# Attention, a token mixer and two feed-forward stages on one core: widening's transfers on GpSimd's queue, and seven weight slabs in attention

## The chip, the core and the metric

The kernel runs on one core of a Trainium2 chip. The metric is the device time of one execution in microseconds (us). Before the change the median of three runs was 990.18 us (990.01 to 993.89). The engines are called TensorE (PE in the rows), VectorE (DVE), ScalarE (ACT), GpSimd (POOL) and SyncE (SP). SP computes nothing, and its queue issues transfers. A row called PEld is TensorE's weight load, which runs beside its matmuls.

## What is computed

The reference is a random-feature attention, a token mixer with a first MLP, and a Fourier mixer with a normalised second MLP. Cut to what matters:

```python
# attention: q, k, v are (4, 8, 576, 64), omega is (128, 64)
phi(x) = exp(h - max(h)) / sqrt(128),  h = x @ omega.T - |x|^2 / 2,  x = x / 64 ** 0.25
kv, z  = sum over s of phi(k) v,  sum over s of phi(k)
x      = (phi(q) kv) / (phi(q) z + 1e-6)                  # as (4, 576, 512)
# mixer and first MLP: w_ch1 is (512, 1536), w_ch2 is (1536, 512)
u      = x + (relu(x^T w_tok1) w_tok2)^T
y      = u + relu(u w_ch1) w_ch2
# Fourier mixer and second MLP: (512, 2048) and (2048, 512)
u      = y + real(fft over features of fft over tokens of y)
out    = u + relu(norm(u) w_ch1') w_ch2'
```

The weights of the token mixer and of both MLPs arrive as 64-bit floating point numbers. The engines work in 32 bits, so the kernel first turns each weight into a high and a low 32-bit part. This step is called widening.

## The kernel before

**Stages.** Attention works through 72 slots, one for each half of a tile of 128 tokens of k or q. In a slot TensorE projects (line 411), VectorE takes a maximum (the reduce of line 425) and ScalarE an exponential (429, 433). Three slots later TensorE adds a k tile to its sums (445) or transposes a q tile (464), and later forms the quotient's numerator (482), which VectorE divides (491 to 505). Once all q tiles of a batch are through, the token mixer's pieces run in the slots as filling: two long ones (15 matmuls each, line 570, and VectorE's line 574 behind them) and eight short ones (line 583, and VectorE's line 586). Seven more slots let the pipeline run out. Then come five blocks of the first MLP (`ch_block`, 12 steps each) and five of the second (`ff_block`, 16 steps each). A step multiplies up (12 matmuls, line 691), takes the relu and its low part (lines 772 and 773) and multiplies the step before down (12 matmuls, line 812 or 1117).

**Weights.** There are 12 slabs of the first MLP and 16 of the second, each 1 MB in and 1 MB out. Widening takes a slab through seven VectorE instructions and one of ScalarE: `take` (273), the scaling on ScalarE (280), `rest` (284), `size` (288), `high` (292), `low` (296), `unit` (300) and `scaled` (304). A load brings a slab from DRAM into one of two buffers (`stg`, line 262). A store takes the result from one of two buffers (`cvo`) to DRAM (`kept`, line 335). A step of an MLP block then loads the slab from there (`w<-kept`, `refill`, line 660) into one of five places, some three steps before it is needed. Four chunks of the token mixer's weights go through the same widening ahead of the slabs.

**The order.** It is written out by hand: each engine runs its instructions in the order in which the program emits them, and each queue its transfers. `Side.step(budget)` stands at the end of every slot and every MLP step. It adds a budget, in microseconds, to a credit and emits widening instructions as long as the credit covers their listed price (6.38 for a slab). `Side.later` puts off a load or store by `defer` steps, four in attention and one after it. All these transfers, and the loads of q, k, v and the slabs, are on SP's one queue, in which a transfer that waits holds up all behind it.

Of the kernel before, what the change touches and what calls it, by code (L numbers as in the profile page):

```python
# [9 lines left out]
F32 = mybir.dt.float32  # L10
# [22 lines left out]

SLOT0_US, SLOT1_US, SLOT_US, FIRST_US, SHORT_US, CH_US, FF_US, SAVED_US = 0.4, 0.65, 0.85, 4.2, 1.2, 3.9, 3.9, 4.5


LAG, LAG_NUM, LAG_X, AHEAD_LOAD, AHEAD_SPLIT, DEFER = 3, 5, 7, 6, 4, 4
# [145 lines left out]
class Side:  # L185
# [10 lines left out]

    def later(self, fn, steps=None):
        due = self.steps + (steps or self.defer)
        k = sum(d <= due for d, _ in self.issues)
        self.issues.insert(k, (due, fn))  # L200

# [33 lines left out]
def mix_kernel(ctx: ExitStack, tc: tile.TileContext, qt, kt, va, om, w1, w2, wch, wff, t1, t2, out):  # L235
    nc = tc.nc
    pe, act, dve, pool, sync = nc.tensor, nc.scalar, nc.vector, nc.gpsimd, nc.sync
# [13 lines left out]
    def widen(src, n, done):  # L251
# [4 lines left out]
        st = {}  # L256
# [2 lines left out]

        def load():  # L260
            st["w"] = cv.tile([128, 2048], I32, tag=f"stg{k}", name="stg")
            sync.dma_start(out=st["w"][:, 0:2 * n], in_=src)

        def take():
            while "w" not in st or k in busy:
# [37 lines left out]
        def scaled():  # L303
            dve.scalar_tensor_tensor(out=st["o"][:, 1, 0:n], in0=st["l"].bitcast(F32), scalar=2.0 ** -52,
                                     in1=st["y"], op0=ALU.mult, op1=ALU.mult)

        f = n / 1024
        return (load, lambda: (done(st), busy.remove(k))), [
            (w * f, fn) for w, fn in ((0.68, take), (0.68, rest), (0.69, size), (1.21, high), (1.21, low), (0.69, unit),
                                      (1.22, scaled))]  # L310
# [18 lines left out]
    kept = {}  # L329
    whole = set()  # L330

    def slab(ff, j):
        def store(st):
            kept[ff, j] = dram.tile([128, 2, 1024], F32, name="kept")
            sync.dma_start(out=kept[ff, j], in_=st["o"].bitcast(F32))
            whole.add((ff, j))
        return widen((wff if ff else wch)[j].bitcast(I32), 1024, store)

# [40 lines left out]
    src = {}  # L379
# [227 lines left out]
        qn, kn = qe, ke  # L607

    side = Side()

    fill = []
    early = []
# [146 lines left out]
    p0.close()  # L759
    ps0.close()  # L760
    pools["S"] = ctx.enter_context(tc.tile_pool(name="ps_s", bufs=2, space=PSUM, reuse_waits="tile")), 2
    side.defer = 1


    hp = ctx.enter_context(tc.tile_pool(name="hp", bufs=2, reuse_waits="tile"))
# [404 lines left out]
```

## Time and profile before

| | before |
|---|---|
| median of three runs | 990.18 us |
| the profiled execution | 989.0 us, of which the span is 987.2 us |
| TensorE busy | 954.3 us (97%) |
| VectorE, ScalarE, GpSimd busy | 551.7, 277.0 and 78.4 us |
| attention with its run-out | the first 210.4 us |
| first block of the first MLP | 210.4 to about 299 us |

The span runs from the first to the last instruction. Busy time is what an engine's instructions took, waits not counted. TensorE is busy nearly all the time, so a change of the whole time shows as a change of TensorE's idle time, or of its clock, or of how many matmuls it is given. The releaser of an idle time is the work whose end let the engine go on.

### The profile page before, as it was taken

What the parts mean: (1) busy time and instruction counts of PE and PEld (TensorE: products, weight loads), DVE (VectorE), ACT (ScalarE), POOL (GpSimd) and SP (SyncE); (2) the same over time, 40 slices, a digit from 0 to 9 for tenths busy, and PEclk for the clock granted to TensorE, in tenths of its full rate; (3) what the DMA queues carried; (4) which work ended last, traced back from release to release, by engine and by line L of the source; (5) the groups of instructions that cost most, each with busy time, mean ns of one, the idle gap of its engine ahead of it and who ended that gap; (6) DMA issues with size and microseconds to landing.
All of it is one profiled execution on the core that took longest, in us unless ns stands there. A gap on an engine that the chain in (4) does not pass through costs nothing.

```text
span 987.2 us, 13163 instructions
## 1 busy us (share of the span) xinstructions
PE 954.3 (97%) x5248; PEld 827.6 (84%) x5248; DVE 551.7 (56%) x1055; ACT 277.0 (28%) x621; POOL 78.4 (8%) x68
## 2 busy tenths in 40 slices
PE   7999999999879899999999999999999999999998
PEld 7999989888759887888888888888888888888897
DVE  6997879696655568966786542154336433511221
ACT  6876667532112212221221211111111111111111
POOL 3443334210000000000000000000000000000000
PEclk9999999999979999999999999999999999999999
DMA  8954433377787779548176673024202420251081
GB/s 281 285 199 146 156 128 139 128 280 263 255 275 270 293 277 422 201 167 328 54 273 219 242 289 128 1 88 169 86 1 86 171 86 1 86 192 64 1 321 41
DMA packets 33693, 175.00 MB, mean 177 GB/s; under 512 B 3680, under 2 KB 4064, under 8 KB 15584
## 3 DMA queue, kind: packets, MB, share of 16 engines
q1 hardware_dynamic: 33488, 173.05, 48.2%
q0 software_dynamic: 144, 1.11, 0.4%
q8 instruction: 41, 0.67, 0.3%
q14 instruction: 20, 0.16, 0.0%
HBM read 136.27 MB, written 34.08 MB: 173 GB/s over the span
## 4 chain that ended last, share of the span: by engine, by line
PE 81%; DMA 9%; DVE 7%; ACT 2%; issue 1%; SPq 0%; POOL 0%; DVEq 0%; ACTq 0%; POOLq 0%
PE H L691 32%; PE A L1117 20%; PE A L812 12%; DMA kept<-cvo 5%; PE A L411 3%; PE A L570 2%; PE N L482 2%; PE H L445 2%; DMA w<-kept 2%; PE S L982 1%; DVE mx L425 1%; ACT f L429 1%; DVE x L495 1%; DMA stg<-in_wch_dram 1%; PE S L995 1%
## 5 line engine op out<-in xcount | busy, mean ns | idle before, releaser
L691 PE MATMUL H<-uh,w 128*128 128x512 f32 (+1 forms) x1120 | 345.5, 375 | 13.1 <-DMA w<-kept 12.3
L691 PEld LDWEIGHTS H<-uh,w 128*128 128x128 f32 x1120 | 207.4, 191 | 49.9 <-DMA w<-kept 13.4
L773 DVE SCALAR_TENSOR_TENSOR hl<-H,hh 128x512 fp32r<-128x512 f32 (+1 forms) x140 | 89.0, 636 | 253.7 <-ACT hh L772 253.3
L772 ACT ACTIVATE hh<-H 128x512 fp32r<-128x512 f32 (+1 forms) x140 | 77.7, 555 | 499.4 <-PE H L691 497.3
L691 PE MATMUL H<-ul,w 128*128 128x512 f32 (+1 forms) x560 | 208.2, 372 | 0.0
L1117 PE MATMUL A<-w,hh 128*128 128x512 f32 x576 | 146.9, 391 | 0.0
L1117 PEld LDWEIGHTS A<-w,hh 128*128 128x128 f32 x576 | 106.6, 188 | 21.0
L691 PEld LDWEIGHTS H<-ul,w 128*128 128x128 f32 x560 | 107.0, 191 | 17.1
L812 PE MATMUL A<-hh,w 128*128 128x512 f32 (+1 forms) x480 | 109.2, 370 | 0.0
L812 PEld LDWEIGHTS A<-hh,w 128*128 128x128 f32 x480 | 85.0, 190 | 15.2
L1117 PE MATMUL A<-w,hl 128*128 128x512 f32 x288 | 80.6, 390 | 0.0
L1117 PEld LDWEIGHTS A<-w,hl 128*128 128x128 f32 x288 | 54.1, 188 | 11.4
L429 ACT ACTIVATE f<-A,mx 128x128 f32<-128x128 f32 x204 | 59.1, 388 | 8.5 <-DVE mx L425 8.2
L812 PE MATMUL A<-hl,w 128*128 128x512 f32 (+1 forms) x240 | 59.3, 369 | 2.1 <-DVE hl L773 2.1
L425 DVE TENSOR_REDUCE mx<-A 128x4 f32<-128x512 f32 x71 | 48.1, 682 | 5.9 <-PE A L411 5.6
L812 PEld LDWEIGHTS A<-hl,w 128*128 128x128 f32 x240 | 42.5, 189 | 10.3 <-DVE hl L773 2.9
L280 ACT ACTIVATE cvy<-cvy 128x1024 f32<-128x1024 f32 (+2 forms) x32 | 32.8, 1025 | 44.0 <-DVE cvy L273 44.0
L445 PE MATMUL H<-v,f 128*128 128x65 f32 x320 | 41.3, 273 | 0.8 <-ACT kvs L450 0.6
L292 DVE SCALAR_TENSOR_TENSOR cvo<-cvy,cvo 128x1024 int32<-128x1024 int32 (+2 forms) x32 | 41.7, 1305 | 0.4
L482 PE MATMUL N<-kvs,qpT 128*128 128x65 f32 x320 | 39.9, 270 | 1.7 <-ACT f L429 0.9
L445 PEld LDWEIGHTS H<-v,f 128*128 128x128 f32 x320 | 40.0, 194 | 1.2 <-ACT kvs L450 0.7
L482 PEld LDWEIGHTS N<-kvs,qpT 128*128 128x128 f32 x320 | 38.6, 192 | 2.4 <-issue 1.7
(182 smaller groups left out, 1150.4 us busy)
## 6 DMA issues: line engine op xcount, KB each, us to landing
w<-kept SPq DMA_DIRECT2D x84, 1024.0 KB, 4.9
kept<-cvo SPq DMA_DIRECT2D x28, 1024.0 KB, 9.1
stg<-in_wff_dram SPq DMA_DIRECT2D x16, 1024.0 KB, 8.7
stg<-in_wch_dram SPq DMA_DIRECT2D x12, 1024.0 KB, 5.2
v<-in_va_dram SPq DMA_DIRECT2D x20, 260.0 KB, 3.7
ks<-in_kt_dram SPq DMA_DIRECT2D x18, 256.0 KB, 3.8
qs<-in_qt_dram SPq DMA_DIRECT2D x18, 256.0 KB, 3.4
out_dram<-U SPq DMA_DIRECT2D x16, 256.0 KB, 2.2
```

The lines of the kernel that those rows point to most:

```text
L280: act.mul(out=st["y"], in_=st["y"], mul=2.0 ** -112)
L292: dve.scalar_tensor_tensor(out=st["h"], in0=st["y"].bitcast(I32), scalar=-0x80000000, in1=st["h"], op0=ALU.bitwise_and, op1=ALU.bitwise_or)
L411: pe.matmul(out=pj[:, p_ * 256:p_ * 256 + 256], lhsT=a[:, c, :], rhs=w, start=(n == 0), stop=(n == 2), skip_group_check=True)
L425: dve.tensor_reduce(out=mx, in_=p4, axis=AX.X, op=ALU.max, negate=True)
L429: act.activation(out=f[:, hh], in_=p4[:, hh], func=AF.Exp, bias=mx[:, hh])
L445: pe.matmul(out=kvp[b, g][:, hh * 65:hh * 65 + 65], lhsT=ft["k", i, g][:, hh, :], rhs=src["v", i, int(off > 0)][:, 4 * g + hh, :], start=( ...
L482: pe.matmul(out=nm[:, hh * 65:hh * 65 + 65], lhsT=t[:, hh, :], rhs=kvs[b, g][:, hh, :], start=(c == 0), stop=(c == len(ts) - 1), skip_grou ...
L691: pe.matmul(out=hb[:, 0:n], lhsT=a[:, kk * 128:kk * 128 + 128], rhs=u[:, kk, 0:n], start=(c == 0), stop=(c == 11))
L772: act.activation(out=hh, in_=hb[:, 0:n], func=AF.Relu)
L773: dve.scalar_tensor_tensor(out=hl, in0=hb[:, 0:n], scalar=0.0, in1=hh, op0=ALU.max, op1=ALU.subtract)
L812: pe.matmul(out=acc[i][:, 0:cols], lhsT=a[:, cs], rhs=v, start=(j == 0 and c_ == 0), stop=(j == NCH - 1 and c_ == 2))
L1117: pe.matmul(out=acc[t], lhsT=a[:, t * 128:t * 128 + 128], rhs=w, start=(j == 0 and c_ == 0), stop=(j == NFF - 1 and c_ == 2))
```

## The change

Three things are changed. The budgets of a slot are now 0.7 (first ten slots), 0.4 (up to the 36th) and 1.2 (after it) instead of 0.4, 0.65 and 0.85; the budget of a step of the MLPs is 3.9 in the first block and 3.7 later instead of 4.2 and 3.9, and at most 4.0 is saved up instead of 4.5. Once attention is emitted, widening's loads and stores go to GpSimd's queue. And from there on they are no longer put off: `later` with a `defer` of zero emits at once.

```diff
-SLOT0_US, SLOT1_US, SLOT_US, FIRST_US, SHORT_US, CH_US, FF_US, SAVED_US = 0.4, 0.65, 0.85, 4.2, 1.2, 3.9, 3.9, 4.5
+SLOT0_US, SLOT1_US, SLOT_US, FIRST_US, SHORT_US, CH_US, FF_US, SAVED_US = 0.7, 0.4, 1.2, 3.9, 1.2, 3.7, 3.7, 4.0
...
     def later(self, fn, steps=None):
         due = self.steps + (steps or self.defer)
+        if due <= self.steps:
+            return fn()
...
-            sync.dma_start(out=st["w"][:, 0:2 * n], in_=src)
+            side.queue.dma_start(out=st["w"][:, 0:2 * n], in_=src)
...
-            sync.dma_start(out=kept[ff, j], in_=st["o"].bitcast(F32))
+            side.queue.dma_start(out=kept[ff, j], in_=st["o"].bitcast(F32))
...
     side = Side()
+    side.queue = sync
...
-    side.defer = 1
+
+    side.defer, side.queue = 0, pool
```

TensorE's instructions stand in the same order in both kernels. Line numbers after the change are higher by 2 to 4. Names end in a number that counts emissions.

**SP's queue in the first block of the first MLP.** Before, from the loads of slabs 2 to 5 on:

```order
L660 DMA w_2870<-kept_2826 128x2048
L262 DMA stg_2881<-in_wch_dram 128x2048
L335 DMA kept_2883<-cvo_2667 128x2048
L660 DMA w_2918<-kept_2883 128x2048
L262 DMA stg_2995<-in_wch_dram 128x2048
L335 DMA kept_2997<-cvo_2831 128x2048
L660 DMA w_3034<-kept_2997 128x2048
L262 DMA stg_3045<-in_wch_dram 128x2048
L335 DMA kept_3047<-cvo_2941 128x2048
L660 DMA w_3083<-kept_3047 128x2048
```

After, the same place:

```order
L337 DMA kept_2758<-cvo_2343 128x2048
L663 DMA w_2892<-kept_1929 128x2048
L663 DMA w_2894<-kept_2118 128x2048
L663 DMA w_2896<-kept_2339 128x2048
L663 DMA w_2898<-kept_2547 128x2048
L663 DMA w_2944<-kept_2758 128x2048
L663 DMA w_3005<-kept_2856 128x2048
L663 DMA w_3059<-kept_2910 128x2048
L663 DMA w_3110<-kept_2974 128x2048
```

Before, each slab's load from `kept` stood between the store of that slab and the store of the next; now only loads from `kept` are left in the row.

**GpSimd's queue behind attention.** Before, one transfer (the Fourier tables) followed the last subtraction of attention:

```order
L512 TENSOR_TENSOR xl_2633<-x_2623,xh_2632 128x512
L512 TENSOR_TENSOR xl_2708<-x_2698,xh_2707 128x512
L512 TENSOR_TENSOR xl_2768<-x_2758,xh_2767 128x512
L845 DMA t2_sb_3410<-in_t2_dram 128x2176
L1166 UNCONDITIONAL_BRANCH
```

After, the loads (`stg`) and stores (`kept`) of widening stand there, 40 in all:

```order
L514 TENSOR_TENSOR xl_2726<-x_2716,xh_2725 128x512
L514 TENSOR_TENSOR xl_2790<-x_2780,xh_2789 128x512
L264 DMA stg_2854<-in_wch_dram 128x2048
L337 DMA kept_2856<-cvo_2551 128x2048
L264 DMA stg_2861<-in_wch_dram 128x2048
L337 DMA kept_2910<-cvo_2794 128x2048
L264 DMA stg_2971<-in_wch_dram 128x2048
L337 DMA kept_2974<-cvo_2859 128x2048
```

They moved here from SP; the first store on this queue is that of the eighth slab.

**VectorE in attention, slots 48 to 50.** The instructions of widening are those with `cvo` or `cvy` on the left. Before:

```order
L425 TENSOR_REDUCE mx_1637<-A_1620 128x4
L425 TENSOR_REDUCE mx_1675<-A_1650 128x4
L292 SCALAR_TENSOR_TENSOR cvo_1494<-cvy_1493,cvo_1494 128x1024
L586 TENSOR_TENSOR x2_652<-A_1688,x2_652 128x288
L425 TENSOR_REDUCE mx_1709<-A_1698 128x4
L432 TENSOR_TENSOR df_1712<-A_1698,mx_1709 128x512
L296 SCALAR_TENSOR_TENSOR cvo_1494<-cvo_1494,stg_1379 128x1024
L425 TENSOR_REDUCE mx_1736<-A_1718 128x4
```

After:

```order
L427 TENSOR_REDUCE mx_1637<-A_1620 128x4
L294 SCALAR_TENSOR_TENSOR cvo_1530<-cvy_1529,cvo_1530 128x1024
L427 TENSOR_REDUCE mx_1674<-A_1649 128x4
L298 SCALAR_TENSOR_TENSOR cvo_1530<-cvo_1530,stg_1456 128x1024
L588 TENSOR_TENSOR x2_657<-A_1689,x2_657 128x288
L427 TENSOR_REDUCE mx_1710<-A_1699 128x4
L434 TENSOR_TENSOR df_1713<-A_1699,mx_1710 128x512
L302 TENSOR_SCALAR cvy_1529<-cvo_1530 128x1024
L275 TENSOR_SCALAR cvy_1719<-stg_1686 128x1024
L427 TENSOR_REDUCE mx_1740<-A_1722 128x4
```

In the same three slots two instructions of widening became four. Counted over VectorE's whole order, widening has 7 instructions before the eleventh reduce, 27 from there to the 37th, and 40 from there to the first MLP's first relu before the change, and 12, 19 and 56 after it; a slab is seven of them.

## Rows read from the trace of the kernel before

**Rows 1.** The page: busy us, share of the span and instructions by engine.

```profile
PE 954.3 (97%) x5248; PEld 827.6 (84%) x5248; DVE 551.7 (56%) x1055; ACT 277.0 (28%) x621; POOL 78.4 (8%) x68
```

**Rows 2.** Busy us (instructions) by stretch; last TensorE's granted clock, DMA share, GB/s.

```profile
core 0: us, PE busy (x) PEld busy (x) DVE busy (x) ACT busy (x) POOL busy (x), PEclk, DMA share, GB/s
0.00:26.80 26.80, 21.13 (x159) 20.57 (x159) 19.03 (x29) 17.22 (x47) 9.76 (x13) 1.00 0.82 284
26.80:85.30 58.50, 55.83 (x456) 54.67 (x457) 50.13 (x93) 46.85 (x131) 26.55 (x22) 0.97 0.71 225
85.30:210.40 125.10, 118.77 (x916) 112.70 (x916) 100.62 (x208) 80.08 (x192) 41.28 (x32) 1.00 0.40 145
210.40:299.00 88.60, 79.09 (x342) 65.32 (x341) 55.88 (x75) 15.61 (x23) 0.52 (x2) 0.92 0.80 280
```

**Rows 3.** TensorE's waits for transfers: 210.5 to 300 us, then 300 to 345 us.

```profile
PE H L691 <- DMA w<-kept: 9.5, 3, 3.7
...
PE H L691 <- DMA w<-kept: 2.8, 2, 1.7
```

**Rows 4.** TensorE in order of time (start, us; idle before): steps 8 to 11.

```profile
259.51 0.40 PE L691 MATMUL H<-uh,w 128*128 128x512 f32 x1
...
262.25 1.98 PE L812 MATMUL A<-hh,w 128*128 128x512 f32 x8
...
269.38 0.80 PE L691 MATMUL H<-uh,w 128*128 128x512 f32 x1 [3.45 <-DMA w<-kept]
...
274.66 2.45 PE L812 MATMUL A<-hh,w 128*128 128x512 f32 x8
...
281.22 0.51 PE L691 MATMUL H<-uh,w 128*128 128x512 f32 x1 [2.40 <-DMA w<-kept]
...
285.49 2.17 PE L812 MATMUL A<-hh,w 128*128 128x512 f32 x8
...
293.04 0.80 PE L691 MATMUL H<-uh,w 128*128 128x512 f32 x1 [3.67 <-DMA w<-kept]
...
297.30 0.42 PE L583 MATMUL S<-w2hl,h1h 128*128 128x288 f32 x2
```

**Rows 5.** SP's queue in order of time (start and us of the issue).

```profile
240.20 0.32 SPq L660 DMA_DIRECT2D w<-kept  x1
...
241.09 0.38 SPq L335 DMA_DIRECT2D kept<-cvo  x1
252.88 0.32 SPq L660 DMA_DIRECT2D w<-kept  x1
```

**Rows 6.** SP's waits over the span: total us, times, longest.

```profile
SPq L660 <- DMA kept<-cvo: 71.2, 8, 11.6
```

**Rows 7.** VectorE busy (instructions) by stretch, of instructions on `cvo` alone.

```profile
0.00:26.80 26.80, 7.39 (x8) 1.00 0.82 284
26.80:85.30 58.50, 21.28 (x22) 0.97 0.71 225
85.30:210.40 125.10, 37.81 (x34) 1.00 0.40 145
```

**Rows 8.** Chain that ended last (start, us), 85.3 to 210.4 us: widening's first and last.

```profile
92.56 0.87 DVE cvo L284
...
204.88 1.69 DVE cvo L284
```

**Rows 9.** VectorE's longest wait, 85.3 to 210.4 us.

```profile
DVE h1l L574 <- ACT h1h L573: 14.1, 6, 3.5
```

**Rows 10.** VectorE at the start: second reduce, first instruction of widening.

```profile
8.16 0.68 DVE L425 TENSOR_REDUCE mx<-A 128x4 f32<-128x512 f32 x1
11.16 0.50 DVE L273 TENSOR_SCALAR cvy<-stg 128x640 f32<-128x640 f32 x1 [2.31 <-DMA stg<-in_w_dram]
```

**Rows 11.** GpSimd's one transfer: its issue, and (page) us to landing.

```profile
298.56 0.69 POOL L845 DMA_DIRECT2D t_sb<-in_t_dram  x1 [88.08 <-PE S L583]
...
t_sb<-in_t_dram POOLq DMA_DIRECT2D x1, 1088.0 KB, 6.1
```

## The prediction

> **What bounds the kernel now.** I read the table of engines first. TensorE is busy 97% of the span, and its 954.3 us leave 33 us [rows 1]. Its instructions keep their order, so the change can only move those 33 us and the time lost to a lower granted clock. The busy time by stretch then tells where they lie [rows 2] (26.8 and 85.3 us are the eleventh and the 37th reduce, where a slot's budget changes): 5.7 us before 26.8 us (the start), 2.7 us up to 85.3 us, 6.3 us from there to the end of attention at 210.4 us, and 9.5 us in the first block of the first MLP, the one stretch whose granted clock is well below full, 0.92. TensorE's waits name the last: three waits for a slab, 9.5 us in all, the longest 3.7 us, and two more in the second block, 2.8 us [rows 3].
>
> TensorE in order of time shows what such a wait costs beyond itself [rows 4]. Twelve matmuls up take 2.74 us in step 8 (259.51 to 262.25). Behind the three waits the same twelve take 5.28, 4.27 and 4.26 us: the clock has fallen to its lower level, 1.2 GHz, in the idle time, and is back at 2.4 GHz some microseconds later. That is 2.54 + 1.53 + 1.52 = 5.6 us more.
>
> Why the slabs are late is in SP's queue [rows 5]. At 240.20 us it issues a slab's load; the load of new weights and the store of the next slab follow, at 241.09 us. The next entry loads that very slab, so it waits until the store has landed, and goes at 252.88 us: 11.8 us later. The store behind it can't go sooner. So one slab comes every 11.8 us, where a step without a wait takes 6.4 us (259.51 to 269.38, less the wait of 3.45 [rows 4]). SP stood 71.2 us, in eight waits, in this way [rows 6].
>
> **The change part by part.**
>
> *The queue.* GpSimd's queue takes the stores and the loads of new weights; SP keeps the loads from `kept`. GpSimd has nothing else to do by then (0.52 us busy in that block [rows 2]). A slab's load may still wait for its store on SP, but no store waits behind it. By the order, the load of slab 11 is now emitted in step 7 and not in step 10, slab 10 in step 6 and not 9, slab 9 in step 5 and not 7. Four steps of 6.4 us lie between slab 11's load and its use, against an 11.8 us store and a load.
>
> *Slabs sooner.* When the first relu of the MLP is emitted, widening has done 87 instructions against 74. Thirteen more of seven each are 1.9 slabs, or 22 us of head start at the old pace. That is more than the 9.5 us by which the slabs are late. So either part alone nearly cures the three waits, and I take them as gone: -9.5 us, and -5.6 us for the clock. In the second block GpSimd's transfers compete with seven slab loads in 12 short steps. The 2.8 us may go or stay; I take half, -1.4 us.
>
> *What it costs in attention.* Thirteen more instructions of widening are on VectorE there, and they aren't spread evenly. An instruction on `cvo` takes 7.39 / 8 = 0.92 us in the first stretch, 21.28 / 22 = 0.97 us in the second and 37.81 / 34 = 1.11 us in the third [rows 7].
>
> First stretch: 12 instead of 7, +4.6 us on a VectorE with little idle time once the weights are there. And the first of them now stands ahead of the second reduce. It waits for its weights until 11.16 us, while that reduce ran at 8.16 us [rows 10]; the reduce would end at about 12.3 us instead of 8.84, 3.4 us later. TensorE is three slots ahead of what it needs from the reduces, which covers part. Ends: nothing, and 4.6 + 3.4 = 8.0 us. I take +2.5 us, nearer to nothing, since matmuls are queued ahead.
>
> Second stretch: 19 instead of 27, -7.7 us. But TensorE stands only 2.7 us there, and its clock of 0.97 over 58.5 us is 1.8 us more [rows 2]. So between nothing and -4.5 us; I take -2.5 us, about half.
>
> Third stretch: 56 instead of 40, +17.8 us. VectorE is busy 100.6 of 125.1 us [rows 2] and would be at 118.4. It has 24.5 us of idle time, of which 14.1 us are six waits behind the token mixer's long pieces [rows 9]: slack, but in six places. Between them VectorE and TensorE go in step. The chain of waits runs through widening there in 17 pieces, 16.2 us in all, from 92.56 to 204.88 us [rows 8]; 16 more on 40 lengthen these by 0.4, or +6.5 us. Ends: +2 us, if the idle time takes nearly all, and +17.8 us, if none. I take +7.5 us, a little above the scaled chain, because a fuller VectorE is on the chain more often.
>
> Sum: -9.5 - 5.6 - 1.4 + 2.5 - 2.5 + 7.5 = -9.0 us. The profiled execution of 989.0 us would take 980.0 us; its span is 1.8 us shorter than that, and the median of the runs 1.2 us longer. On the median of 990.2 us it is 981.2 us. The rest of the MLPs I cost at nothing: TensorE never waits for a slab there, budgets fall by 0.2, and 1.9 slabs are already done.
>
> A rule weighed against the change: SP's rows show a queue whose head waits while transfers behind it are ready, and here 11.8 us a slab hang on that [rows 5]. The Trainium skill, "DMA: Bandwidth & Descriptors", section "Issuing engines are not separate DMA queues", says that transfers from several engines run on the same 16 DMA engines, and that issuing from several saves only the issue time. By it the move alone would bring next to nothing, and the sum would rest on the head start; the sum is then the same, since 22 us cover the waits.
>
> **The rivals.**
>
> *Attention pays in full.* VectorE's idle time is latency and not slack: each added microsecond delays TensorE. Price: 17.8 + 8.0 - 2.5 = +23.3 us, against 9.5 + 5.6 saved and nothing in the second block: +8.2 us, 998.4 us. It turns slower once attention pays over 15.1 us. For it: the chain passes through widening seventeen times in the third stretch. Against it: the 14.1 us behind the long pieces, and TensorE itself at 118.8 of 125.1 us, so that at present it is VectorE that has the room.
>
> *Attention pays almost nothing.* The six waits and TensorE's own queue take the added work (+2), the start nothing, the second stretch gives 4.5 and the second block 2.8: -9.5 - 5.6 - 2.8 + 2 - 4.5 = -20.4 us, 969.8 us.
>
> *GpSimd's queue is slow.* Each of its transfers waits for VectorE. The one such transfer shown was issued in 0.69 us and landed in 6.1 us for 1.06 MB [rows 11], which speaks against it; but then VectorE wasn't in the midst of widening. Price: with a step's four widening instructions of some 0.92 us (the first stretch's mean) ahead of each transfer, two transfers a slab are 7.4 us late; the last four slabs eat the head start of 22 us and the slack. Part of the three waits returns, some 5 us with their clock: -4 us, 986 us. Where it also starves VectorE of new weights all 15.1 us return: +6 us, 996 us. The Trainium skill, "SBUF — State Buffer", section "SBUF: two separate sides", has this as a trap: while VectorE runs certain fast copies, GpSimd can't write its transfers' descriptors, and such transfers belong on SP's or ScalarE's queue. No row here shows a store from GpSimd.
>
> *The change doesn't do what it says.* Excluded by the order: 40 transfers stand in GpSimd's queue, and slab 11's load is three steps sooner.
>
> **How the numbers follow.** The forecast, with its terms off by some microseconds (976 to 987 us): 0.60. Almost nothing paid: 0.12. Paid in full or nearly (990 to 999 us): 0.14. GpSimd slow (984 to 996 us): 0.14. The range of 8 in 10 runs from 970.5 to 991 us: it holds the forecast, most of the cheap case and the milder half of the other two. A measurement of this kernel tells about 0.5% from no change, so 985.2 and 995.1 us are the bounds. Faster: nearly all of 0.60, 0.12 and a part of the slow queue, 0.72. Slower: over half of the full price, 0.09. Within: 0.19.
>
> **What would show it.** TensorE's waits for slabs in the first two blocks fall from 12.3 us to under 3 us, and the granted clock of the first block is at 0.99 or more. SP no longer waits eight times for a store. Attention ends at about 218 us instead of 210.4, with VectorE at 93% or more in its third stretch. It would be wrong in its main step if attention ended after 226 us, or if the waits for slabs stayed above 5 us, and in its sizes if attention ended before 213 us.

## The result

The changed kernel takes 979.12 us (median of 14 runs, 973.77 to 989.8), the kernel before, on the same chip, 992.07 us (14 runs, 987.04 to 994.4). The ratio is 0.9869, 95% interval 0.9845 to 0.9893: 1.3% faster, some 13 us. Here and below, medians and extremes are over all runs, while the ratios leave out runs over 1.5% above the fastest of the same kernel (two each of the changed kernel, e2 and e8). The forecast was 981.2 us, 9 us under the kernel before. The profiled execution of the changed kernel took 977.99 us, with a span of 975.9 us; before it was 989.0 and 987.2 us.

The page of the changed kernel, first the busy times, to be held against [rows 1]:

```profile
PE 952.6 (98%) x5248; PEld 828.6 (85%) x5248; DVE 549.0 (56%) x1055; ACT 277.1 (28%) x621; POOL 110.3 (11%) x108
```

TensorE does the same 5248 matmuls in nearly the same busy time; GpSimd has 108 instructions instead of 68, the 40 transfers that moved. The span is 11.3 us shorter. I cut both spans at places that can be found in both traces: the first matmul of step 1 of the first block, the first matmul of the second block, that of the third block, and the end. These starts are read from TensorE in order of time.

| stretch | before, us | after, us | difference | forecast |
|---|---|---|---|---|
| start to step 1 of the first block (attention) | 210.43 | 217.91 | +7.5 | +7.5 |
| first block, from step 1 | 93.13 | 76.81 | -16.3 | -15.1 |
| second block | 37.92 | 38.06 | +0.1 | -1.4 |
| from the third block to the end | 645.7 | 643.1 | -2.6 | 0 |
| span | 987.2 | 975.9 | -11.3 | -9.0 |

TensorE's waits of after, from 195 to 345 us (total us, times, longest), answer to [rows 3]:

```profile
PE H L694 <- DMA w<-kept: 2.7, 3, 1.6
```

These three are all in the second block. In the first block there is none. Its stretch in after (us, then busy us of TensorE, of its weight loads, VectorE, ScalarE and GpSimd, then the granted clock, the DMA share and GB/s) is to be held against the last of [rows 2]:

```profile
217.50:297.00 79.50, 79.50 (x385) 67.26 (x384) 58.71 (x83) 16.89 (x28) 14.07 (x17) 1.00 0.83 314
```

In this stretch TensorE is busy 79.50 of 79.50 us at a granted clock of 1.00, where it was 0.92 before.

The waits of SP's queue over the span, which answer to [rows 6], and GpSimd's for a store:

```profile
SPq L663 <- PE A L816: 249.1, 35, 33.5
...
SPq L663 <- DMA kept<-cvo: 24.9, 3, 11.2
```

```profile
POOL kept L337 <- DVE cvo L306: 138.5, 21, 29.8
```

The longest waits of SP's loads of slabs are now for a free place, that is for the matmuls of a slab's last use (L816), 249.1 us, where it was 186.7 before: more slabs are there before they can be loaded. It waits for a store 24.9 us in three waits, where it was 71.2 us in eight. The time that a transfer of widening waits for VectorE has gone to GpSimd, where nothing else stands behind it but the next one of widening.

The transfers by issue (count, KB each, median us from issue to landing) show whether GpSimd's queue costs anything beyond the one transfer of [rows 11]. First after, then before:

```profile
kept<-cvo POOLq DMA_DIRECT2D x21, 1024.0 KB, 7.4
stg<-in_wff_dram POOLq DMA_DIRECT2D x16, 1024.0 KB, 6.5
...
kept<-cvo SPq DMA_DIRECT2D x7, 1024.0 KB, 4.6
```

```profile
kept<-cvo SPq DMA_DIRECT2D x28, 1024.0 KB, 9.1
stg<-in_wff_dram SPq DMA_DIRECT2D x16, 1024.0 KB, 8.7
```

A megabyte from GpSimd lands in 6.5 to 7.4 us, with VectorE widening beside it. From SP's queue before, the same loads took 8.7 us and the stores 9.1, so the move made neither slower. The seven stores that still go from SP, in 4.6 us, are all in attention, where less is moved (a DMA share of 0.40 in its last stretch, against 0.80 in the first block [rows 2]); they can't be held against the 7.4.

### The profile page after: what moved, and what is told of

Its sections match the earlier page's. It is cut to its first block, busy times and chain, and to the rows that moved or that the text cites. A ratio compares the mean times of both kernels' runs of the same rounds, so it can differ in the third digit from the quotient of the medians.

```text
span 975.9 us, 13168 instructions
## 1 busy us (share of the span) xinstructions
PE 952.6 (98%) x5248; PEld 828.6 (85%) x5248; DVE 549.0 (56%) x1055; ACT 277.1 (28%) x621; POOL 110.3 (11%) x108
## 4 chain that ended last, share of the span: by engine, by line
PE 88%; DVE 7%; DMA 2%; ACT 1%; issue 1%; SPq 0%; DVEq 0%; ACTq 0%
PE H L694 35%; PE A L1121 20%; PE A L816 15%; PE A L413 3%; PE N L484 2%; PE H L447 2%; PE A L572 2%; PE S L986 1%; DVE mx L427 1%; DMA w<-kept 1%; DVE x L497 1%; PE S L999 1%; DVE cvo L298 1%; PE S L585 1%; PE S L1105 1%
## 5 line engine op out<-in xcount | busy, mean ns | idle before, releaser
L694 PE MATMUL H<-uh,w 128*128 128x512 f32 (+1 forms) x1120 | 341.1, 371 | 2.7 <-DMA w<-kept 2.7
L694 PEld LDWEIGHTS H<-uh,w 128*128 128x128 f32 x1120 | 205.0, 189 | 37.9 <-DMA w<-kept 3.3
L816 PE MATMUL A<-hh,w 128*128 128x512 f32 (+1 forms) x480 | 108.6, 368 | 0.0
L816 PEld LDWEIGHTS A<-hh,w 128*128 128x128 f32 x480 | 84.3, 189 | 14.8
L816 PE MATMUL A<-hl,w 128*128 128x512 f32 (+1 forms) x240 | 59.1, 368 | 0.0
L816 PEld LDWEIGHTS A<-hl,w 128*128 128x128 f32 x240 | 42.7, 189 | 7.5
L484 PE MATMUL N<-kvs,qpT 128*128 128x65 f32 x320 | 42.4, 280 | 2.6 <-DVE x L507 2.6
L484 PEld LDWEIGHTS N<-kvs,qpT 128*128 128x128 f32 x320 | 41.2, 202 | 3.1 <-POOL ql L401 2.4
L306 DVE SCALAR_TENSOR_TENSOR cvo<-cvo,cvy 128x1024 fp32r<-128x1024 f32 (+2 forms) x32 | 40.0, 1250 | 0.0
L294 DVE SCALAR_TENSOR_TENSOR cvo<-cvy,cvo 128x1024 int32<-128x1024 int32 (+2 forms) x32 | 38.9, 1214 | 0.5
```

Of the source, the lines that this page charges most:

```text
L294: dve.scalar_tensor_tensor(out=st["h"], in0=st["y"].bitcast(I32), scalar=-0x80000000, in1=st["h"], op0=ALU.bitwise_and, op1=ALU.bitwise_or)
L484: pe.matmul(out=nm[:, hh * 65:hh * 65 + 65], lhsT=t[:, hh, :], rhs=kvs[b, g][:, hh, :], start=(c == 0), stop=(c == len(ts) - 1), skip_grou ...
L694: pe.matmul(out=hb[:, 0:n], lhsT=a[:, kk * 128:kk * 128 + 128], rhs=u[:, kk, 0:n], start=(c == 0), stop=(c == 11))
L816: pe.matmul(out=acc[i][:, 0:cols], lhsT=a[:, cs], rhs=v, start=(j == 0 and c_ == 0), stop=(j == NCH - 1 and c_ == 2))
```

## The experiments

In every run the time before was taken again on the same chip: 992.47 us beside e1 to e4, 991.62 beside e5 to e8, 991.36 beside e9 to e12. "Step 1" is the start of the twelve matmuls up of step 1 of the first block, "first block" the time from there to the first matmuls of the second; both, and the waits for slabs in that stretch, are from the profiled execution (e12's is the slowest of its ten). The waits of 10.3 and 16.0 us that the expectations of e5 and e12 name are those of e1 and e4 with the second block's added.

| kernel | median, us (runs) | ratio, 95% interval | step 1, us | first block, us | its waits for slabs, us |
|---|---|---|---|---|---|
| before | 992.07 (14) | 1 | 210.4 | 93.1 | 9.5 |
| after | 979.12 (14) | 0.9869, 0.9845 to 0.9893 | 217.9 | 76.8 | 0 |
| e1: queue alone | 981.88 (4) | 0.9874, 0.9831 to 0.9918 | 212.0 | 85.5 | 7.0 |
| e2: shares alone | 988.48 (10) | 0.9944, 0.9911 to 0.9978 | 217.8 | 82.5 | 2.1 |
| e3: queue alone, put off | 981.61 (4) | 0.988, 0.9837 to 0.9923 | 212.0 | 84.3 | 4.6 |
| e4: at once, on SP | 989.04 (10) | 0.9955, 0.9937 to 0.9974 | 212.3 | 95.1 | 12.8 |
| e5: third share back | 1004.27 (4) | 1.0138, 1.0066 to 1.021 | 215.3 | 101.0 | 17.7 |
| e6: old shares, steeper block | 972.8 (4) | 0.9812, 0.977 to 0.9853 | 209.1 | 79.5 | 1.2 |
| e7: between | 973.97 (4) | 0.9815, 0.9778 to 0.9852 | 215.7 | 76.8 | 0 |
| e8: stores on SP | 988.71 (9) | 0.9957, 0.9929 to 0.9985 | 215.9 | 86.5 | 7.6 |
| e9: three slots free | 974.47 (4) | 0.9823, 0.9789 to 0.9856 | 216.4 | 76.8 | 0 |
| e10: after again | 979.44 (6) | 0.9869, 0.9835 to 0.9903 | 217.8 | 76.8 | 0 |
| e11: e6 again | 974.78 (4) | 0.9833, 0.98 to 0.9866 | 210.4 | 77.5 | 0 |
| e12: e6 on SP | 995.21 (10) | 1.0031, 1.0011 to 1.0052 | 213.3 | 102.3 | 8.3 |

### The two parts apart (e1 to e4)

The change has two parts, the queue (with transfers put off by no step) and the shares. Theory A, that of the prediction, was that either part alone nearly cures the waits in the first block. The first kernel has the queue alone. Against the changed kernel:

```diff
-SLOT0_US, SLOT1_US, SLOT_US, FIRST_US, SHORT_US, CH_US, FF_US, SAVED_US = 0.7, 0.4, 1.2, 3.9, 1.2, 3.7, 3.7, 4.0
+SLOT0_US, SLOT1_US, SLOT_US, FIRST_US, SHORT_US, CH_US, FF_US, SAVED_US = 0.4, 0.65, 0.85, 4.2, 1.2, 3.9, 3.9, 4.5
```

> The old budgets stay, and only the queue and the immediate emission are taken over. Theory A (each part alone nearly cures the late slabs, and the budgets' price is paid in attention): attention ends at about 210 us as before, TensorE waits under 3 us for slabs in the first block, and the time is 15 to 18 us under the kernel before, 6 to 8 us under the changed one. Rival B (the head start does it, the queue is nothing because all transfers share the same engines): the three waits stay near 9.5 us and the time is within 4 us of the kernel before.

Measured: 981.88 us, some 11 us under before, and one wait of 7.0 us left in the first block, for slab 11. That is between Theory A, which had under 3 us of waits and 15 to 18 us, and Rival B. Attention, at step 1, is where it was before, within 2 us. SP, GpSimd and TensorE of this kernel in order of time (start, us; GpSimd's and TensorE's rows end with the idle time before them) show why that one is left:

```profile
268.14 11.62 SPq L663 DMA_DIRECT2D w<-kept  x2
```

```profile
271.85 0.53 POOL L337 DMA_DIRECT2D kept<-cvo  x1 [1.31 <-DVE cvo L306]
```

```profile
287.09 0.79 PE L694 MATMUL H<-uh,w 128*128 128x512 f32 x1 [7.01 <-DMA w<-kept]
```

The slab's store is issued at 271.85 us, 1.31 us after GpSimd began to wait for VectorE. SP issues two loads between 268.14 and 279.76, the second of them when that store has landed. The load lands 7.3 us later. No queue held it up: its widening was finished late. (Its two transfers took their time too, 7.5 and 7.6 us; how much of the 7.0 us is theirs was not separated.) The load of slab 11 is emitted in step 9 here, in step 7 in the changed kernel.

The second kernel has the shares alone, everything on SP and put off by one step. Against the kernel before:

```diff
-SLOT0_US, SLOT1_US, SLOT_US, FIRST_US, SHORT_US, CH_US, FF_US, SAVED_US = 0.4, 0.65, 0.85, 4.2, 1.2, 3.9, 3.9, 4.5
+SLOT0_US, SLOT1_US, SLOT_US, FIRST_US, SHORT_US, CH_US, FF_US, SAVED_US = 0.7, 0.4, 1.2, 3.9, 1.2, 3.7, 3.7, 4.0
```

> The new budgets alone; widening's transfers stay on SP and are put off by one step as before. Theory A: attention ends some 7.5 us later, at about 218 us, the waits for slabs in the first block fall to 0 to 6 us (at 11.8 us a slab the last of them comes about 5 us late), and the time is 3 to 9 us under the kernel before. Rival C (the queue does it all): attention ends at 218 us and the waits stay at 9.5 us or more, so the time is 5 to 9 us over the kernel before.

Measured: 988.48 us, as Theory A had it. The first block gains 10.6 us, and attention gives 7.4 of that back. Beside the waits for slabs, 2.1 us, TensorE waits 2.4 us there for VectorE's halves of the activations.

The third kernel is the queue alone, put off by one step as before; the fourth puts off by no step, but on SP. Against the changed kernel, both with the old shares as in the first kernel, and

```diff
-    side.defer, side.queue = 0, pool
+    side.defer, side.queue = 1, pool
```

> Old budgets, GpSimd's queue, but loads and stores still put off by one step. Theory A (what counts is that no store waits behind a slab's load): waits for slabs 0 to 5 us, the time 10 to 17 us under the kernel before. Rival D (the immediate emission does it): the loads of slabs 9 to 11 are emitted as late as before, in steps 7, 9 and 10, so 5 us or more of the waits stay, and the time is under 9 us less than before.

```diff
-    side.defer, side.queue = 0, pool
+    side.defer, side.queue = 0, sync
```

> Old budgets, all on SP's queue, but emitted at once. Theory A: every slab's load still holds up the store behind it, one slab in about 11.8 us; the waits fall only by what the start gains, to 4 to 9 us, and the time is 1 to 8 us under the kernel before. Rival D: the waits vanish, 15 us under.

Measured: 981.61 and 989.04 us. Putting off makes no difference that can be seen on GpSimd (981.88 against 981.61): Theory A holds in e3, and Rival D falls. On SP the first block gets longer, with a wait of 8.57 us in step 2, and the median is still a little lower. Theory A's time for e4 came out, but not its waits (4 to 9 us, measured 12.8), and what held the slabs up is something else than it named. SP in order of time, in the fourth kernel:

```profile
206.75 0.32 SPq L337 DMA_DIRECT2D kept<-cvo  x1
215.88 0.33 SPq L264 DMA_DIRECT2D stg<-in_wch_dram  x1
218.22 0.32 SPq L337 DMA_DIRECT2D kept<-cvo  x1
218.64 3.46 SPq L663 DMA_DIRECT2D w<-kept  x4
```

A store emitted at once stands at the head of SP's queue until VectorE has finished the slab. Four loads stand behind it. They go together as soon as the store has gone, at 218.64 us.

What follows: the queue alone brings 10.6 us by the medians and 12.5 by the ratio, the shares alone 4.0 and 5.6, and both together 13. They don't add up, since they take the same waits away and only the shares cost anything in attention. The intervals of the queue alone (0.9831 to 0.9918) and of both (0.9845 to 0.9893) overlap all the way: that the shares add anything to the queue is not shown. Theory A's "either alone nearly cures" falls: the queue alone takes 7.6 of the first block's 16.3 us, the shares alone 10.6.

### Which of the transfers has to leave SP (e8)

The changed kernel with the stores on SP and the loads of new weights on GpSimd:

```diff
-            side.queue.dma_start(out=kept[ff, j], in_=st["o"].bitcast(F32))
+            sync.dma_start(out=kept[ff, j], in_=st["o"].bitcast(F32))
```

> The changed kernel with the stores of widened slabs on SP again; only the loads of new weights go through GpSimd. Theory A (what the queue move cures is a store standing behind a slab's load that waits, on SP): SP waits for stores for 35 us or more, 3 to 6 us of waits for slabs come back in the first block, and 981 to 988 us, near the run with the new shares and everything on SP (988.5). Rival B (what mattered were the loads of new weights, which stood behind SP's waiting head and kept VectorE from widening): no wait for a slab in the first block, 977 to 981 us as the changed kernel.

Measured: 988.71 us, and one wait for a slab of 7.56 us in step 2. The time is Theory A's within a microsecond; its sign on SP is not. SP in order of time, TensorE's wait, and SP's waits over the span:

```profile
217.07 0.32 SPq L337 DMA_DIRECT2D kept<-cvo  x1
217.49 4.37 SPq L663 DMA_DIRECT2D w<-kept  x4
```

```profile
229.87 0.80 PE L694 MATMUL H<-uh,w 128*128 128x512 f32 x1 [7.56 <-DMA w<-kept]
```

```profile
SPq L663 <- PE A L816: 174.2, 36, 27.9
SPq L337 <- DVE cvo L306: 146.6, 24, 20.8
...
SPq L663 <- DMA kept<-cvo: 14.8, 3, 8.5
```

SP waits for stores to land for only 14.8 us, not the 35 that I had expected. But it waits 146.6 us for VectorE to finish what a store is to take, up to 20.8 us, and four loads are issued right behind such a store at 217.49. So the stores have to leave SP, at least where they are emitted at once; moving the loads of new weights alone brought nothing beside what the shares bring (a ratio of 0.9957 here, 0.9944 with the shares alone). Yet the loads' move did cure what it was for: before the change VectorE waited 17.6 us, in five waits from 209 us on, for new weights that stood in SP's queue, and here 0.8 us. Not tried, and so not shown, is whether moving the stores alone is enough, whether stores on SP do better put off by a step with the loads moved, and whether another free queue than GpSimd's would serve as well.

### Is the head start needed (e6, e11, e7, e12)

What was left with the queue alone was a slab widened too late in the block. So the next kernel keeps attention's old shares, and widens faster in the block instead. From the kernel with the queue alone it differs in two numbers only, 5.2 us a step for 4.2 and up to 5.2 us saved for 4.5. Against the changed kernel:

```diff
-SLOT0_US, SLOT1_US, SLOT_US, FIRST_US, SHORT_US, CH_US, FF_US, SAVED_US = 0.7, 0.4, 1.2, 3.9, 1.2, 3.7, 3.7, 4.0
+SLOT0_US, SLOT1_US, SLOT_US, FIRST_US, SHORT_US, CH_US, FF_US, SAVED_US = 0.4, 0.65, 0.85, 5.2, 1.2, 3.9, 3.9, 5.2
```

> Stores and loads of widening on GpSimd's queue and put off by no step, as changed, but the three stretches of attention keep the shares of before (0.4, 0.65, 0.85); instead the first block gives widening 5.2 us a step, not 4.2, with 5.2 us savable. The loads of slabs 7 to 11 are then emitted in steps 3, 4, 5, 6, 7 as in the changed kernel. Theory A (a slab is late only where its widening is paced too slowly in the block; the head start from attention is one way to get it, and not needed): step 1 at 210 to 213 us, waits for slabs in the first block at most 2 us, granted clock there 0.99 or more, 970 to 976 us. Rival B (VectorE can't take 5.2 us of widening in a step of 6.4 us beside the splits and relus, or GpSimd's transfers can't keep that pace, so the head start is needed): waits for slabs or for VectorE of 5 us or more in the first block, 978 to 983 us.

Measured: 972.8 us. Step 1 starts at 209.1 us, the waits for slabs in the first block are 1.2 us. The first block in this kernel (columns as above):

```profile
209.00:288.60 79.60, 77.81 (x363) 64.65 (x362) 67.08 (x92) 17.75 (x26) 16.41 (x21) 1.00 0.90 343
```

VectorE is at 67.08 of 79.60 us, 84%, and TensorE keeps its clock. So Theory A holds (step 1 came a little sooner than it said), and the head start isn't needed. SP's waits of this kernel add something:

```profile
SPq L663 <- DMA kept<-cvo: 71.9, 8, 11.5
```

That is what the kernel before had, 71.2 us in eight waits [rows 6], in a kernel that is 19 us faster. These waits cost nothing by themselves; they cost what stands behind them.

The same kernel again, beside the changed kernel again:

> The kernel with the old shares in attention, GpSimd's queue, and 5.2 us of widening a step in the first block, once more. If attention's price is avoided and not moved, as one look at it said (972.8 us), it is 971 to 975 us and 3 to 8 us under the changed kernel of this call. If that was chance, it is 977 us or more.

> The changed kernel, unchanged, beside the others of this call, to compare them on one chip: 976 to 981 us, ratio 0.985 to 0.989.

Measured: 974.78 and 979.44 us, 4.7 us apart. The order of the two is the same as between their first runs; the intervals of their ratios, 0.98 to 0.9866 and 0.9835 to 0.9903, overlap, so the size of the difference is not well known.

Half way between the two, with a third share of 1.0 and 4.8 us a step in the block. Against the changed kernel:

```diff
-SLOT0_US, SLOT1_US, SLOT_US, FIRST_US, SHORT_US, CH_US, FF_US, SAVED_US = 0.7, 0.4, 1.2, 3.9, 1.2, 3.7, 3.7, 4.0
+SLOT0_US, SLOT1_US, SLOT_US, FIRST_US, SHORT_US, CH_US, FF_US, SAVED_US = 0.4, 0.65, 1.0, 4.8, 1.2, 3.9, 3.9, 4.8
```

> As the run with 5.2 us a step and the old attention, but half way: 0.4, 0.65 and 1.0 in attention, 4.8 us a step in the first block; slabs 7 to 11 are loaded in steps 3 to 7 again, and the widening ahead of the first block is 80 or so pieces. Theory A (attention's price grows with the share of the third stretch): step 1 at 213 to 215 us, no wait above 1 us for a slab in the first block, 973 to 978 us. Rival B (the third stretch has a point from which it pays: the six places with idle time take what is added up to there): step 1 at 210 to 212 us, no low clock near 176 us, 971 to 975 us.

Measured: 973.97 us, step 1 at 215.7 us, no wait in the first block. The time is in Theory A's span, and in Theory B's too; step 1 is beyond either's, so the run doesn't tell them apart by the time, and speaks against both in attention, as far as one profiled execution can: the cost of the third stretch doesn't grow in step with its share (it takes 114.9 us at 1.0, 114.1 to 116.6 at 1.2 and 107.9 to 109.4 at 0.85), and a low clock near 176 us is there (0.75 from 170 to 180 us). TensorE's two long waits there, in order of time:

```profile
129.01 0.50 PE L572 MATMUL A<-xh,w1hl 128*128 128x512 f32 x1 [2.05 <-ACT f L431]
174.87 3.60 PE L484 MATMUL N<-kvs,qpT 128*128 128x65 f32 x16 [1.83 <-POOL ql L401]
```

Last the steeper block on SP. Against the kernel with 5.2 us a step:

```diff
-    side.defer, side.queue = 0, pool
+    side.defer, side.queue = 0, sync
```

> The kernel with the old shares in attention and 5.2 us a step in the first block, but with widening's loads and stores on SP, put off by no step. Theory A (on SP a load of a slab that waits for its store, or for a free place, stands ahead of the next store and of the next new weights, so no pace in the block helps): 8 to 16 us of waits for slabs, as on SP with 4.2 us a step (16.0), and 984 to 990 us. Rival B (the pace alone is what was short): waits under 5 us, 972 to 978 us.

Measured: 995.21 us, 0.1 to 0.5% slower than before. The waits for slabs are 8.3 us in the first block, and VectorE's and ScalarE's halves of the activations now come late too, as TensorE's waits from 195 to 360 us show:

```profile
PE H L694 <- DMA w<-kept: 10.3, 3, 8.3
PE A L816 <- DVE hl L777: 4.7, 3, 3.8
PE A L816 <- ACT hh L776: 3.1, 1, 3.1
```

Both theories expected it faster than before. Theory A is right that no pace helps on SP, but its price is too low, and its mechanism is not all of it. The one wait for a slab in the first block, in step 2, is like those of e4 and e8: a store goes out at 219.28 us, once VectorE has finished the slab, and four loads right behind it. From step 8 on it is as Theory A has it, but TensorE pays in another way: new weights stand on SP behind a slab's load that waits for its store, VectorE stands for the new weights, and the halves of the activations stand behind that piece in VectorE's order:

```profile
287.76 0.69 DVE L275 TENSOR_SCALAR cvy<-stg 128x1024 f32<-128x1024 f32 x1 [4.53 <-DMA stg<-in_wff_dram]
```

So a faster pace in the block pays with the transfers on GpSimd's queue, and not on SP's.

### What attention pays for (e5, e9)

The changed kernel with the third share back at 0.85:

```diff
-SLOT0_US, SLOT1_US, SLOT_US, FIRST_US, SHORT_US, CH_US, FF_US, SAVED_US = 0.7, 0.4, 1.2, 3.9, 1.2, 3.7, 3.7, 4.0
+SLOT0_US, SLOT1_US, SLOT_US, FIRST_US, SHORT_US, CH_US, FF_US, SAVED_US = 0.7, 0.4, 0.85, 3.9, 1.2, 3.7, 3.7, 4.0
```

> The changed kernel with one budget back: 0.85 instead of 1.2 a slot in the third stretch of attention; first and second stretch, queue and deferral as changed. Theory A (the third stretch is what attention pays for): the twelve matmuls of step 1 start at 210 to 213 us instead of 218.1, and the 2.2 us wait near 176 us with the low clock behind it is gone. In exchange the loads of slabs 7 to 11 are emitted in steps 4, 6, 7, 9, 10, later than with the queue alone (3, 4, 6, 8, 9, where the waits were 10.3 us), so 10 to 16 us of waits for slabs return: 983 to 990 us. Rival B (the price is paid in the first stretch, where 12 pieces stand instead of 7 and the second reduce ran 3.3 us later): step 1 stays at 216 us or later, and the time is above 988 us.

Measured: 1004.27 us, far above Theory A's time and above Rival B's bound, and step 1 at 215.3 us, between the two theories, so attention pays in both places. The wait near 176 us was still there (2.51 us at 175.85). The first block takes 101.0 us, with two waits for slabs, 17.7 us in all, the second for slab 11:

```profile
304.42 0.79 PE L694 MATMUL H<-uh,w 128*128 128x512 f32 x1 [11.50 <-DMA w<-kept]
```

The shares of attention add up to 7 + 10.4 + 30.6 = 48.0 us here (10 slots of 0.7, 26 of 0.4, 36 of 0.85), against 51.5 with the old shares and 60.6 with the new; and the block goes at 3.9 us a step, not 4.2. With less done ahead and a slower pace the first block takes 24 us longer than in the changed kernel.

Where attention pays can be read from the reduces of VectorE, of which there is one a slot, 72 in all. The rows of the kernel before at the eleventh, the 37th and the last:

```profile
23.30 0.68 DVE L425 TENSOR_REDUCE mx<-A 128x4 f32<-128x512 f32 x1
...
80.12 0.68 DVE L425 TENSOR_REDUCE mx<-A 128x4 f32<-128x512 f32 x1
...
188.04 0.68 DVE L425 TENSOR_REDUCE mx<-A 128x4 f32<-128x512 f32 x1
```

and of the changed kernel:

```profile
28.43 0.68 DVE L427 TENSOR_REDUCE mx<-A 128x4 f32<-128x512 f32 x1
...
79.48 0.68 DVE L427 TENSOR_REDUCE mx<-A 128x4 f32<-128x512 f32 x1
...
196.07 0.68 DVE L427 TENSOR_REDUCE mx<-A 128x4 f32<-128x512 f32 x1
```

So the first stretch costs 5.1 us, the second gives 5.8 back (51.05 against 56.82), and the third costs 8.7 (116.59 against 107.92). Over all profiled executions the first ends at 28.4 to 31.4 us with the new share (six of them, mean 29.4) and at 23.3 to 23.7 with the old (eight, mean 23.5); the second takes 51.1 to 53.5 (mean 52.0) against 55.2 to 58.4 (mean 56.6); the third 114.1 to 116.6 at 1.2 (four, mean 115.1) against 107.9 to 109.4 at 0.85 (the seven with the old shares ahead of it, mean 108.7).

The changed kernel's third stretch has one long wait of TensorE. It and the clock around it:

```profile
176.60 2.84 PE L484 MATMUL N<-kvs,qpT 128*128 128x65 f32 x16 [2.22 <-DVE x L507]
```

```profile
170.00:175.00 5.00, 3.48 (x29) 1.00 0.52 193
175.00:180.00 5.00, 3.40 (x20) 0.75 0.36 151
180.00:190.00 10.00, 10.00 (x58) 0.61 0.10 40
190.00:200.00 10.00, 10.00 (x61) 1.00 0.34 119
```

What VectorE did ahead of that, in order of time:

```profile
172.86 0.83 DVE L302 TENSOR_SCALAR cvy<-cvo 128x1024 int32<-128x1024 int32 x1
173.62 0.88 DVE L275 TENSOR_SCALAR cvy<-stg 128x1024 f32<-128x1024 f32 x1
174.41 0.67 DVE L427 TENSOR_REDUCE mx<-A 128x4 f32<-128x512 f32 x1
175.01 0.15 DVE L493 TENSOR_SCALAR rd<-N 128x8 f32<-128x8 f32 x1
```

Two pieces of widening stand ahead of the reduce and the division that TensorE waits for. So in the last experiment widening gets nothing in three slots there. Against the changed kernel:

```diff
-                side.step(SLOT0_US if n < 10 else SLOT1_US if n < 36 else SLOT_US)
+                side.step(SLOT0_US if n < 10 else SLOT1_US if n < 36 else 0.0 if 63 <= n < 66 else SLOT_US)
```

> The changed kernel, with widening given nothing in the slots 63 to 65 of attention, so that the four pieces that VectorE ran between 168 and 175 us, ahead of the division at 175.0, come later. Theory A (a good half of what the third stretch costs is one wait: TensorE stood 2.22 us at 176.60 us for that division, and its clock then was low for some 10 us, a loss of 5 us): the wait there falls under 1.3 us, the granted clock is 1.00 from 170 to 190 us, step 1 of the first block starts at 210 to 214 us instead of 217.9, and the time is 972 to 976 us. Rival B (VectorE has no room, and the wait only moves to the next place where two pieces fall together): a wait of 1.8 us or more elsewhere between 150 and 200 us, step 1 at 216 us or later, 977 to 981 us.

Measured: 974.47 us. The wait at that place is 0.44 us, and the clock stays (the same stretches of this kernel):

```profile
170.00:175.00 5.00, 5.00 (x46) 1.00 0.40 161
175.00:180.00 5.00, 4.56 (x41) 1.00 0.01 2
180.00:190.00 10.00, 9.55 (x83) 1.00 0.29 107
```

The third stretch takes 109.53 us here, against 116.59 and 114.05 in the two profiled executions of the changed kernel. That is 7.1 and 4.5 us less. The wait of 2.2 us, less 0.44, and the clock lost behind it (5.2 us in the one execution, 1.7 in the other) are 7.0 and 3.5 us of it. So most of the 8.7 and 6.1 us that the stretch cost hung on this one place: Theory A holds in its mechanism and its time, and no wait of Rival B's size turned up elsewhere. It is not that four pieces fewer stand in this attention (83 ahead of the first relu, 87 in the changed kernel): the kernel with a third share of 1.0 has 81, and its third stretch took 114.9 us. What counts is where the pieces fall. The same matmul waits 0.86 us in the kernel before (at 172.74 us), 2.22 in the changed one, 2.51 with the third share back at 0.85, 1.83 at 1.0 and 0.44 here. Its step 1, expected at 210 to 214 us, came at 216.4, because this execution lost more at the start, where the eleventh reduce came at 31.37 us. That is the other place where the clock falls, in this kernel:

```profile
15.00:20.00 5.00, 3.83 (x19) 0.65 0.56 159
20.00:25.00 5.00, 5.00 (x25) 0.50 0.46 135
25.00:30.00 5.00, 5.00 (x26) 0.50 1.03 331
```

In the changed kernel, with the same share there, it was back sooner, 0.71 from 15 to 20 us and 0.95 from 20 to 25. In the kernel before, with the old share, it is 1.00 there [rows 2].

## Why the prediction was right, point by point

**The bound.** TensorE, its idle time, and above all the first block: right. The stretch gave 16.3 us, of which attention took 7.5 back. All of it is waits and clock: its granted clock went from 0.92 to 1.00, and its matmuls' busy time from 83.6 us to 76.8.

**The three waits and their clock.** Forecast -9.5 and -5.6, measured -16.3 together. Right for the two parts together. The step ahead of it, "either part alone nearly cures the three waits", was wrong: of the 9.5 us of waits and the 16.3 us of the block's time, the queue alone left 7.0 and 8.7 us, the shares alone 2.1 and 5.7. The clock's part is 6.8 us (83.6 less 76.8), not 5.6, because I had counted only the matmuls up behind each wait. I had counted the queue's 11.8 us a slab as the pace, and forgot that without the queue's waits the pace of widening itself (4.2 us a step) comes next; slab 11's load came in step 9 instead of 7, and TensorE waited 7 us for it.

**Why the slabs were late.** The diagnosis on SP (a store behind a load that waits for a store) was half of it. The stores are what must leave, as the run with stores on SP showed; but the waits of SP for stores, which I took as the sign, were as long in the fastest kernel as before. On the rule of the Trainium skill, "DMA: Bandwidth & Descriptors", section "Issuing engines are not separate DMA queues", that issuing from several engines saves only the issue time: here the move alone, put off as before (e3), gave a ratio of 0.988 (0.9837 to 0.9923), some 11 us, where the 40 issues of 0.32 to 0.38 us [rows 5] that leave SP are about 14 us of SP's time, and none of TensorE's. The sentence says nothing of what stands behind a waiting transfer; here the measurement decides.

**The second block.** Forecast -1.4, measured +0.1: the 2.7 us of waits stayed. The bounds had 0.

**Attention.** Forecast +2.5, -2.5 and +7.5, together +7.5; measured in the profiled executions +5.1, -5.8 and +8.7, with -0.5 behind the last reduce, together +7.5. The sum was right because two errors met. The first stretch was sized too low: "nearer to nothing, since matmuls are queued ahead" failed, because the 2.84 us that VectorE waits for the first weights reach TensorE as waits of 0.5 and 1.3 us, and the clock falls behind them, another 1.7 us. The second was sized beyond its bound, which rested on a false reading: 26.8 and 85.3 us, given as the eleventh and the 37th reduce of the kernel before, are the 13th and the 38th; the true ones are at 23.3 and 80.1 us. And TensorE's idle time within the stretch was no bound: what the first stretch had put off came back in it, so that the two together end at 78.5 to 81.9 us in all but one of the profiled executions (84.9 in e9), whichever share they have. The terms for them should have been one. The third was right in size and wrong in kind: not sixteen pieces that each add a little to a chain, but one place where two pieces fall ahead of a division, a wait of 2.22 us, and 5.2 us of lost clock (0.25 of 5 us and 0.39 of 10).

**The rest.** Forecast nothing, measured -2.6 us. The kernel before had two waits for VectorE's half of the activations there, from 345 to 420 us, which after doesn't have:

```profile
PE A L812 <- DVE hl L773: 2.1, 2, 1.2
```

The chain of waits of before leads from them to VectorE's widening, and from there to stores on SP, for whose landing it waited 11.10 and 9.35 us:

```profile
361.59 11.10 DMA kept<-cvo
372.69 0.02 issue
372.71 0.48 DVE cvo L284
373.19 9.35 DMA kept<-cvo
```

Not only the queue cures this. The kernels with the stores on SP but emitted at once (e4, e8, e12) have no such wait either, and take 643.1 to 643.3 us from the third block to the end; the shares alone, on SP and put off, have one of 1.67 us and take 645.1. So here it is enough either to leave SP or to emit at once. The prediction had looked for TensorE's waits for slabs alone, of which there were none.

**The rivals.** Attention paid 7.5 us, not 23.3 and not -2.5. GpSimd's queue was not slow: a store landed in 7.4 us, where SP's took 9.1 before, and VectorE no longer waited for new weights. On the trap in the Trainium skill, "SBUF — State Buffer", section "SBUF: two separate sides", by which such transfers wait while VectorE runs certain copies: with VectorE busy 58.71 of 79.50 us, mostly with widening, GpSimd's stores still landed in 7.4 us in the median, sooner than SP's before; no run here shows such a stall at a cost to TensorE.

**The signs.** Waits for slabs in the first two blocks under 3 us (2.7), clock 0.99 or more (1.00), and attention ending near 218 us (217.9) came out, and SP waits for a store three times and not eight, though the fastest kernel shows that this sign means little. VectorE at 93% in the third stretch did not come out: from 86.0 to 217.5 us it is busy 111.39 of 131.50 us, 85%. The added pieces brought 10.8 us of busy time there, not 17.8; and by my own sum, which made the stretch 7.5 us longer, the sign should have been 89% (118.4 of 132.6).

## What to carry to other kernels

Look in a queue not for who waits, but for what is ready behind the waiting entry: some 71 us of SP's waits went with 9.5 us of TensorE's in the first block of one kernel and with 1.2 in another, and a store put ahead of four loads cost 8 us. Before you buy a head start with work in a stretch where engines go in step, see whether the block that needs it has room: on GpSimd's queue, 1 us more of widening a step there did what 9 us more in attention did, without its price. And where a filler is spread by a share a slot, look for the one slot where two pieces meet ahead of what TensorE waits for; three slots left free brought the third stretch as low as the whole share put back (109.5 and 111.2 us, one execution each).

## What the runs showed of the hardware

A wait of TensorE can cost more by its clock than by itself, and how much is not the same from one execution to the next. Behind or around each of the 20 waits of 2.2 us or more after its first matmul, in the profiled executions of all kernels, the granted clock was at its lower level for some time. Shorter ones went both ways. Behind one of 2.13 us at 226 us in e2 and one of 1.99 us at 312 us in e6 it stayed at 1.00, and behind one of 2.05 us at 129 us in e7 and one of 1.74 us at 342 us in e12 it fell (0.83 in the 10 us from 130 and from 340 us). Behind one of 1.24 us at 145 us and one of 0.86 us at 172 us, in the kernel before, it stayed at 1.00; behind one of 1.28 us at 107 us it stayed in that kernel and fell in e1 (0.95 and 0.88 in the two stretches of 10 us); behind one of 1.77 us at 53 us it fell in the kernel before (0.83 from 50 to 60 us), and behind the same one of 1.78 us it stayed in e6. The changed kernel lost 5.2 us behind the wait at 176.60 us in one execution, and 1.7 us behind the same one in the other. At the start, waits of 0.5 to 0.9 us (1.75 in e8) and of 1.3 us within 4 us did it too, and there the time at the lower level, worked out from the granted clock by stretch, was 3.4 us in the changed kernel and 17 us in e9. Whether the spread of a kernel's times comes from this was not tried.
